# Hourglass attention and a gated MLP on one core: values by casting transfers, the k sums of batch 0 on TensorE, its norms in two parts

## The chip, the cores and the metric

The kernel runs on one core of a Trainium2 chip. Five engines work side by side from instruction lists of their own: TensorE (PE; its weight loads are listed apart as PEld), VectorE (DVE), ScalarE (ACT), GpSimd (POOL) and SyncE (SP). [...] Transfers run on 16 DMA engines, which all queues share. The metric is the time on the device in microseconds (us): the median of five runs of the kernel before is 329.76 us, with 327.95 as the lowest and 330.70 as the highest.

## The reference

```
q, k, v: 8 batches x 8 heads x 576 positions x 64, float32
q_d, k_d, v_d = means over 4 neighbouring positions (144 positions)
out_d   = softmax(q_d k_d^T / 8) v_d, each row repeated 4 times
out_loc = softmax over |i - j| < 4 of (q k^T / 8), times v
x       = out_d + out_loc, as 4608 tokens x 512
h       = x w_in            (512 -> 2048)
out     = (h * sigmoid(1.702 h)) w_out      (2048 -> 512)
```

So for every batch there are two attentions: one over all of a sequence shortened by four, and one over a band of seven positions. The MLP then takes all heads of a token together.

## The kernel before

The order of every engine is written out by hand: an instruction stands where its line is called, and nothing reorders it. The MLP is cut into nine groups of 512 tokens. A group is `mm1` (16 blocks of 128 hidden units, four matmuls of 128x512 each, L693) and then `mm2` (4 blocks of 128 tokens, 16 matmuls each, L749). While group g runs, the attention of batch g + 1 is put between its matmuls at numbered steps (`POS`, for group 0 `POS_0` and `VDP_0`). Steps from 16 on lie in `mm2`.

Before group 0 there is a lead-in: batch 0 must be loaded, attended and transposed before the first matmul of the MLP can start. It is written out at L787 to L890, and the change lies there and in the loads of batch 1.

- *Loads.* q and k come by DMAs of GpSimd's queue that cast float32 to bfloat16 (`load_1`, L202), 288 KB each as landed. The values of batch 0 come as float32 by ten DMAs of SyncE's queue (`load_v`, L222, two for each of five chunks) into the buffer `vf`, and VectorE casts each chunk into `vb` (`prep_v`, L319). A one-element copy on GpSimd (L812) reads chunk 2 of `vf`, and `w_in` (L255) is issued behind it, then q and k of batch 1, then the first half of `w_out` (L264). For batch 1, chunks 3 and 4 come by casting DMAs (`load_vb`, L233), and chunks 0 to 2 through `vf` with casts on GpSimd, with two more one-element copies as gates (L785, L907).
- *Transposes and sums of four.* VectorE transposes k and q (`prep_1`, L279) into `kT` and `qT`. GpSimd adds four neighbours in two steps (`pool_qk`, L304 and L313) into `kdT` and `qdT`; for the q of the second half of the heads VectorE does it in one reduction (`pool_q_reduce`, L293).
- *Scores.* `scores` (L384) are 80 small matmuls for the band of four heads, laid over a bar that `bar_others` (L365) writes. `scores_d` (L403) are 24 matmuls for the short attention, with `kdT` as the weights. ScalarE takes the exponentials (L414, L420, L832).
- *Averages.* `av_local0` (L523) and `av_down0` (L539) multiply by the values, for a pair of heads each; the values carry a column of ones, so the sums for the norm come along. The short values are sums of `vb` by TensorE (`prep_vd_pe`, L346), copied out by ScalarE (L355). `normalise0` (L552 to L557) is a reciprocal and two products on VectorE. `transp_sum` (L573, L584) transposes and adds the two attentions, and `copy_x` (L597 to L603) moves the result to `xT`.
- *Fillers.* `warm` (L649) are float32 matmuls whose result nobody reads. Each is carried out as two weight loads and two matmuls.
- *Start of the MLP.* `part` (L693) runs the matmuls of the first six hidden blocks as soon as each pair of heads is in `xT`.

PSUM holds three two-bank tiles (`PA[0]` to `PA[2]`) and two one-bank tiles (`PM`).

## Time and profile before

| What | Value |
|---|---|
| Median of 5 runs | 329.76 us |
| Profiled execution | 330.7 us, span 327.9 us |
| TensorE busy | 310.2 us (95%), 4962 weight loads |
| ScalarE, GpSimd, VectorE busy | 185.2, 138.0, 131.5 us |
| Granted TensorE clock | 1.000 of full speed |
| First matmul of hidden block 6 in group 0 (the lead-in is over) | 31.82 us |
| First long run of matmuls of group 1 | 66.16 us |

A busy TensorE is not TensorE at its peak, since the ends of its matmuls are modelled and fillers count as busy. Times in the text are counted from the start of the span. In the chain of waits each piece has a start, a length and what it was; "issue" is time in which an engine waited for nothing that the profile shows. In the list of instructions in order of time, a group has its start, its length, its line, what it wrote and read, and in brackets the idle time ahead of it.

### The profile page before, as it was taken

How to read it: one execution, taken by the hardware profiler on the slowest of the kernel's cores; microseconds unless marked ns; L12 is line 12 of the kernel's file. 1: busy time of each engine (PE TensorE's matmuls, PEld its weight loads, DVE VectorE, ACT ScalarE, POOL GpSimd, SP SyncE). 2: the span in 40 equal slices, each digit the busy share in tenths (PEclk: the TensorE clock that was granted, in tenths of full speed). 3: DMA queues.
4: the chain of work that ended last, by engine and by line, in shares of the span. 5: the costliest groups of instructions: out<-in, count | busy, mean ns of one | idle time of the engine just before them, and what ended most of it. 6: DMA issues, size and time to landing. Idle time of an engine off the chain costs nothing.

```text
span 327.9 us, 11050 instructions
## 1 busy us (share of the span) xinstructions
PE 310.2 (95%) x4908; PEld 159.0 (48%) x4962; DVE 131.5 (40%) x220; ACT 185.2 (56%) x322; POOL 138.0 (42%) x167
## 2 busy tenths in 40 slices
PE   8999979899999999999899999999999999999996
PEld 3564444445554554454544554445444544444444
DVE  6655332750676047703681267217730560000000
ACT  4645881566846582659267745775576646415611
POOL 7883851079306940496029901990098000000000
PEclk9999999999999999999999999999999999999999
DMA  7999999999917990699139942995190110011012
GB/s 125 182 191 209 189 128 196 187 193 252 173 68 153 203 161 36 151 205 185 46 108 184 175 116 72 185 207 125 55 155 3 65 39 32 0 66 64 0 54 75
DMA packets 63551, 41.08 MB, mean 125 GB/s; under 512 B 44048, under 2 KB 54416, under 8 KB 63504
## 3 DMA queue, kind: packets, MB, share of 16 engines
q1 hardware_dynamic: 52944, 26.42, 39.7%
q0 software_dynamic: 10416, 13.90, 25.0%
q8 instruction: 38, 0.62, 0.8%
q14 instruction: 9, 0.07, 0.1%
q10 hardware_dynamic: 144, 0.07, 0.1%
HBM read 44.83 MB, written 9.44 MB: 165 GB/s over the span
## 4 chain that ended last, share of the span: by engine, by line
PE 88%; DVE 5%; issue 4%; DMA 2%; ACT 1%; POOL 0%; ACTq 0%; DVEq 0%; POOLq 0%
PE pm L693 35%; PE pm L749 32%; PE pa L384 4%; PE pa L693 2%; PE pa L403 2%; PE pa L445 2%; PE pa L467 2%; DMA qb<-in_q_dram 2%; PE pa L749 2%; PE pa L498 2%; DVE xT L631 1%; PE pm L649 1%; PE pm L764 1%; DVE y L484 1%; DVE yl L557 1%
## 5 line engine op out<-in xcount | busy, mean ns | idle before, releaser
L693 PE MATMUL pm<-xT,w_in_bf 128*128 128x512 bf16 x528 | 120.3, 379 | 1.6 <-DVE xT L637 0.9
L749 PE MATMUL pm<-w_out_bf,gT 128*128 128x512 bf16 x493 | 114.1, 379 | 5.6 <-issue 5.5
L704 ACT ACTIVATE gT<-pm 128x512 bf16<-128x512 f32 x136 | 81.0, 598 | 46.1 <-PE pm L693 46.1
L693 PEld LDWEIGHTS <-w_in_bf 128*128 128x128 bf16 x576 | 55.6, 98 | 68.1 <-issue 1.9
L749 PEld LDWEIGHTS <-gT 128*128 128x128 bf16 x560 | 51.8, 98 | 59.6 <-issue 0.2
L304 POOL TENSOR_TENSOR pq<-kT 128x576 f32<-128x576 bf16 x16 | 18.5, 1158 | 98.0 <-DVE kT L279 97.9
L428 DVE TENSOR_TENSOR es<-es,mask 128x600 bf16<-128x600 bf16 x28 | 20.9, 762 | 90.3 <-ACT es L414 89.5
L734 ACT ACTIVATE osb<-pm 128x512 f32<-128x512 f32 (+2 forms) x35 | 20.8, 593 | 41.2 <-PE pm L749 37.3
L610 ACT COPY od<-pa 128x384 f32<-128x384 f32 (+1 forms) x56 | 18.4, 413 | 31.4 <-DVE y L484 18.7
L484 DVE TENSOR_TENSOR y<-pa,rc 128x896 bf16<-128x896 f32 x28 | 30.6, 1092 | 1.0
L631 DVE TENSOR_TENSOR xT<-pa,od 128x570 bf16<-128x570 f32 x28 | 21.1, 753 | 11.9 <-ACT od L610 11.5
L325 POOL TENSOR_TENSOR v<-v 112x512 f32<-112x512 f32 x18 | 22.8, 1265 | 0.0
L736 DVE TENSOR_SCALAR osb<-pm 128x128 f32<-128x128 f32 x1 | 0.3, 292 | 55.3 <-ACT osb L734 55.3
L414 ACT ACTIVATE es<-pa 128x600 bf16<-128x600 f32 x32 | 19.7, 668 | 2.5 <-PE pa L384 2.2
L279 DVE STREAM_TRANSPOSE kT<-kb 128x576 f32<-128x576 f32 x16 | 20.0, 1250 | 1.8 <-DMA kb<-in_k_dram 1.8
L279 DVE STREAM_TRANSPOSE qT<-qb 128x576 f32<-128x576 f32 x16 | 19.9, 1243 | 1.8 <-DMA qb<-in_q_dram 1.7
L304 POOL TENSOR_TENSOR pq<-qT 128x576 f32<-128x576 bf16 x15 | 17.2, 1146 | 0.0
L319 POOL CAST vb<-vf 128x2560 bf16<-128x2560 f32 (+1 forms) x9 | 16.1, 1810 | 0.0
L384 PEld LDWEIGHTS <-kT 32*64 32x64 bf16 x1280 | 12.1, 104 | 7.0 <-issue 5.6
L483 DVE RECIPROCAL rc<-pa 128x14 f32<-128x14 f32 x28 | 6.7, 241 | 21.3 <-PE pa L467 21.3
L420 ACT ACTIVATE ed<-pa 128x864 bf16<-128x864 f32 x15 | 13.5, 897 | 2.2 <-PE pa L403 2.2
L384 PE MATMUL pa<-qT,kT 32*64 32x60 bf16 x1280 | 14.1, 203 | 0.3 <-DVE qT L279 0.3
(104 smaller groups left out, 259.2 us busy)
## 6 DMA issues: line engine op xcount, KB each, us to landing
vf<-in_v_dram SPq DMA_DIRECT2D x76, 128.0 KB, 6.5
out_dram<-osb SPq DMA_DIRECT2D x35, 256.0 KB, 2.1
v<-in_v_dram SPq DMA_DIRECT2D x36, 192.0 KB, 5.4
kb<-in_k_dram POOLq DMA_DIRECT2D x16, 288.0 KB, 7.6
qb<-in_q_dram POOLq DMA_DIRECT2D x16, 288.0 KB, 8.8
w_out_bf<-in_moe_w_out_dram POOLq DMA_DIRECT2D x4, 512.0 KB, 13.4
w_in_bf<-in_moe_w_in_dram POOLq DMA_DIRECT2D x2, 512.0 KB, 7.5
w_in_bf<-in_moe_w_in_dram POOLq DMA_DIRECT2D x1, 1024.0 KB, 12.6
```

Of the source, the lines that this page charges most:

```text
L279: nc.vector.transpose(out=t32.rearrange("p (i c) -> p c i", c=18), in_=store[b, qd].bitcast(FP32).rearrange("p (c d) -> p c d", c=18),)
L304: nc.gpsimd.tensor_tensor(out=t1, in0=sv[:, :, 0:2, :], in1=sv[:, :, 2:4, :], op=ALU.add)
L325: eng.tensor_tensor(out=t1[0:112], in0=x[:, :, 0:2, :], in1=x[:, :, 2:4, :], op=ALU.add)
L384: nc.tensor.matmul(sp[r // 2][64 * par : 64 * par + 64, r % 2, 60 * i : 60 * i + 60], lhsT=kT[b, qd][rows, k0 : k0 + 64, a], rhs=qT[b, qd] ...
L414: nc.scalar.activation(out=es[2 * qd + u][:, :, 0:300], in_=sp[u][:, :, 0:300], func=AF.Exp, scale=inv_sqrt_d,)
L428: nc.vector.tensor_tensor(out=ev, in0=ev, in1=mask, op=ALU.mult)
L484: nc.vector.tensor_tensor(out=y[:, xs], in0=ov[:, :, :, 0:D], in1=rc[:, xs].to_broadcast([128, n, 7, D]), op=ALU.mult,)
L631: eng.tensor_tensor(out=sub(xT[hp], t0 + 3, (57, 2), (114, 5), (1, 57)), in0=sub(x, 3, (509, 2), (57, 5), (1, 57)), in1=sub(od, 3, (57, 2) ...
L693: nc.tensor.matmul(acc, lhsT=w_in_bf[:, dmc, ffc * 128 : (ffc + 1) * 128], rhs=xT[dmc][:, g * TG : g * TG + TG], start=(dmc == 0), stop=(d ...
L704: nc.scalar.activation(out=gT[:, ffc, :], in_=acc, func=AF.Silu, scale=GELU_SCALE)
L734: eng.activation(out=osb, in_=ap, func=AF.Copy, scale=1.0 / GELU_SCALE)
L749: nc.tensor.matmul(ops[t], lhsT=gT[:, ffc, t * 128 : (t + 1) * 128], rhs=w_out_bf[:, ffc, :], start=(ffc == 0), stop=(ffc == n_ffc - 1),)
```

## The change

The values of batches 0 and 1 all come by casting DMAs of GpSimd's queue straight into `vb`; `vf`, the casts and the gates of these two batches are gone. In batch 0 the sums of four over k are no longer formed: TensorE multiplies each of the four k rows by the summed q and adds the four products in PSUM (`scores_d0`, 96 matmuls in place of 24). The q sums of batch 0 are both reductions on VectorE. `normalise0` can run in two parts, "a" for the first four columns of results and "b" for the rest. Pairs 0, 1 and 2 are averaged side by side instead of 0 and 1 first, most fillers are taken out, and two steps of group 0 stand earlier.

```diff
+    def scores_d0(qd, sd):
+        bank = banks(sd)
+        for kc in range(3):
+            for a in range(2):
+                for f in range(4):
+                    for r in range(4):
+                        rows = slice(32 * r, 32 * r + 32)
+                        j = r % 2
+                        k0 = 192 * kc + f
+                        nc.tensor.matmul(
+                            bank[r // 2][64 * j : 64 * j + 64, SD * kc : SD * kc + SD],
+                            lhsT=kT[0, qd][rows, k0 : k0 + 253 : 4, a],
+                            rhs=qdT[0, qd][rows, :, a],
+                            start=(a == 0 and f == 0), stop=(a == 1 and f == 3),
+                            tile_position=(32 * r, 64 * j),
+                        )
+        return sd
...
-    POS_0 = [16, 18, 27, 54, 68, 60, 76]
-    VDP_0 = 52
+    POS_0 = [16, 18, 27, 50, 68, 60, 76]
+    VDP_0 = 46
...
-    load_v(0, gate=after(kdT[1][0:1, SD, 0:1], nc.vector))
+    for i in range(5):
+        load_vb(0, i)
+    load_w_in(0, 512)
+    load_w_in(512, 512)
+    load_w_in(1024, 1024)
+    for qd in range(NQ):
+        load_qk(1, qd)
+    load_w_out(0)
+    load_w_out(1)
...
-    pool_qk(0, 0)
-    sp = scores(0, 0, barred=True)
+    sp = scores(0, 0, barred=True, sp=PA[0:2])
     exp_local(0, sp)
     prep_1("k", 0, 1)
+    pool_q_reduce(0, 0)
     prep_1("q", 0, 1)
     pool_q_reduce(0, 1)
-    pool_qk(0, 1, "k")
...
-    for i in range(5):
-        prep_v(0, nc.vector, i=slice(i, i + 1))
     warm(2)
-    sd = scores_d(0, 0)
-    exp_down(0, sd)
-    sp = scores(0, 1, barred=True)
+    exp_down(0, scores_d0(0, PA[2]))
+    sp = scores(0, 1, barred=True, sp=PA[0:2])
     exp_local(1, sp)
-    for hp in range(2):
-        o[hp] = PA[hp]
-    warm(1)
-    scores_d(0, 1, PM)
+    scores_d0(1, PM)
...
+    for i in (range(3), range(3, 4)):
+        for hp in range(3):
+            av_local0(hp, o[hp], i)
+    for hp in range(3):
+        normalise0(o[hp], y[hp], "a")
+    prep_vd_pe(0, PM[0], range(0, 2))
+    prep_vd_pe(0, PM[1], range(2, 3))
     nc.scalar.preload_act_table_set("silu_and_others")
-    warm(1, t=PA[2][:, 0, :])
...
+    for hp in range(3):
         av_local0(hp, o[hp], range(4, 5))
-    prep_vd_pe(0, pm_tile(), range(2, 3))
-    warm(1, 256)
-    for hp in range(2):
+        if hp == 0:
+            warm(1, 256, PM[0])
         av_down0(hp, o[hp])
-        y[hp] = normalise0(o[hp])
...
-    warm(1)
-    warm(1, 256)
+        normalise0(o[hp], y[hp], "b")
+    warm(1, t=PM[0])
...
         if g == 0:
             nc.gpsimd.memset(v4[32:64], 0.0)
+            load_vb(1, 0)
+            load_vb(1, 1)
+            prep_qk(1, 0)
+            pool_qk(1, 0)
+            load_vb(1, 2)
+            prep_qk(1, 1)
+            pool_qk(1, 1)
             load_vb(1, 3)
             load_vb(1, 4)
-            load_v(1, gate=after(qf[1, 1][0:1, 0:1], nc.vector), chunks=range(3))
...
             load_w_out(2)
             load_w_out(3)
-            for i in range(3):
-                prep_v(1, nc.gpsimd, i=slice(i, i + 1))
             for qd in range(NQ):
                 load_qk(2, qd)
-            loads_2()
+            load_v(2, gate=after(w_out_bf[0:1, 12, 0:1], nc.gpsimd))
+            load_v4(2)
```

The k tiles of batch 0 are made 64 positions longer, and VectorE clears the tail, so that the strided weights of `scores_d0` stay inside the tile.

## The prediction

> **What bounds the kernel now.** I began with the page's first part, then the chain of waits in order of time, then TensorE's weight loads and VectorE's list, and last the DMA view in short windows.

> ```profile
> PE 310.2 (95%) x4908; PEld 159.0 (48%) x4962; DVE 131.5 (40%) x220; ACT 185.2 (56%) x322; POOL 138.0 (42%) x167
> ...
> q8 instruction: 38, 0.62, 0.8%
> ```

> TensorE is the bound: from 66.16 us, where group 1 gets going, the chain runs from matmul to matmul. The change leaves that stretch alone. So it can move the end only by moving the lead-in (to 31.82) and group 0 (to 66.16). The lead-in in the chain, with start, length and work:

> ```profile
> 9.57 1.91 PE pm L649 x4
> 11.48 0.51 PE pa L403 x24
> 11.99 0.62 PE pa L365 x4
> 12.61 0.84 PE pa L384 x79
> 13.46 1.05 PE pm L649 x2
> 14.51 0.44 PE pm L403 x17
> 14.95 0.21 issue
> 15.16 0.32 PE pm L403 x7
> ...
> 31.82 0.21 PE pm L693
> ```

> VectorE's norms of the first pairs of heads stand in the list by time:

> ```profile
> 20.98 0.25 DVE L552 RECIPROCAL rc<-pa 128x14 f32<-128x14 f32 x1 [2.83 <-PE pa L539]
> 21.26 0.42 DVE L553 TENSOR_TENSOR yd<-pa,rc 128x256 bf16<-128x256 f32 x1
> 21.60 0.95 DVE L557 TENSOR_TENSOR yl<-pa,rc 128x768 bf16<-128x768 f32 x1
> ```

> Now the pause at 14.95: 0.21 us in the middle of 24 equal matmuls, for nothing. A far longer one lies in group 0:

> ```profile
> 46.49 0.43 PEld L403 LDWEIGHTS <-kdT 32*64 32x64 bf16 x24 [1.74 <-issue]
> ```

> What this line waits for in the code (`kdT`, `qdT`, the exponential that frees PSUM) was done by 44.42. I counted TensorE's weight loads up to each unexplained pause. The pauses at 14.95, 44.66, 60.14, 121.38 and 156.31 (0.21 to 1.8 us) come after 224, 735, 991, 2014 and 2654 loads. From the first they are 511, 767, 1790 and 2430 on: multiples of 128, two off at most. Each load has one matmul, so it is every 256 instructions, and 2 x 4962 instructions over the 38 packets of the instruction queue is 261 per packet. TensorE waits there for its own instruction list.

> In quarter-microsecond windows those packets start at 12.25, 17.5, 24.25, 30.5, 43.25, 51.0, 58.25 and 62.25; TensorE passes block borders (256 instructions) at 11.4, 15.16, 21.0, 27.6, 40.9, 46.49, 54.7 and 60.8. One packet per border, fetched one block ahead. Border to packet takes 2.4, 3.4 and 3.05 us at 15 to 30 us, while weights stream in; packet to release 2.4 to 3.2 us. Where the next border had to wait, border to release was 4.1 (122.07), 4.7 (157.40), 5.6 (46.49) and 6.0 us (60.77).

> [...] the new weights of L403's successor step by 4 positions of 4 bytes, `kdT` by 4 bytes. [...]

> **The change part by part, for the lead-in.**

> *Values.* Ten casting DMAs follow the iotas on GpSimd at 6.33; one issue takes 0.68 (24.86, L233), so the last is out at 13.1. Landed by what? In 38.5 to 39.0 the engines moved 513 such packets, a whole DMA of 512 in 0.48 us, so ten need 4.8 behind q and k (about 8.9): the data is in by about 15, the last landed near 16. TensorE needs chunk 4 after 18. The five casts (0.43 each) leave VectorE. Cost on the path: nothing, 2 us of cover. `w_in` is issued at 13.1 instead of 14.58; batch 1's loads follow about 3 us earlier, also covered: TensorE waited for none of them before. With six values DMAs more, GpSimd still issues the second half of `w_out` by 42.5 (44.6 before).

> *k sums.* Six GpSimd operations go (three of 1.15 + 0.67). VectorE gets a reduction of 1.35 and two small clears: transpose of kT1 to about 10.0, reduction to 11.35. The filler ends at 11.48, so no wait. `scores_d0` is 96 matmuls for 24. Such a piece took 0.51 for 24 and 0.39 for 23 later: 17 to 21 ns each, so 1.6 to 2.0 us, 3.3 if the 16-byte step doubles it; I take 1.8. Twice 1.8 for 0.51 and 0.76 is +2.3.

> *Fillers.* From 13.46 on 1.05, 1.06, 0.84, 0.63, 0.63 and 1.5 go; 0.63 and 1.05 stay: -4.0.

> *Norms.* VectorE's products cost 1.03 ns an element ((0.95 - 0.42)/512). Part "a" is 0.28 + 0.61, "b" 0.27 + 0.34 + 0.34 by starts: 5.5 us for three pairs, 4.4 before, but "a" starts 3.5 us sooner.

> *Without the instruction list* the sum runs: scores_d0 11.5 to 13.3; bar and scores (0.62, 0.84) to 14.8; scores_d0 to 16.6; averages (48 x 16 ns) to 17.4; short values (0.69 + 0.28) to 18.4; VectorE's "a" 17.4 to 20.1, "b" to 23.0; last filler to 21.65; transposes (0.73 each), pair 3 (0.66) and 24 matmuls of 0.216 end at 30.4. That is 1.4 before 31.82. The two earlier steps in group 0 I cost at nothing: the same matmuls, their values in by 43; if late, TensorE would pause by that delay.

> *With it.* The new matmuls are 144 pairs, and five fillers fewer take out 20 instructions: +268 instructions in the lead-in, and where 9.6 us passed between the borders at 11.4 and 21.0, the code now wants 5.6. Border at load 224 is reached at 14.15 (28 pairs into the second scores), released as before at about 15.15: 1.0 lost. The next border lies 76 matmuls into the second scores_d0, reached at 17.1; released 15.15 + 2.4 + 2.4 = 19.95: 2.85 lost. Rest, exponentials, averages and "a" follow; the third lies in the short averages of pair 1, reached at 23.7, released 19.95 + 3.4 + 2.4 = 25.75: 2.05 lost. The fourth lies in pair 3's transposes, reached at 31.8, released at 25.75 + 5.4 = 31.15. From 25.75: rest of pairs 1 and 2 0.5, filler 1.05, transposes, pair 3 and first matmuls 5.0 to 32.2, the last 18 matmuls 3.9: 36.1. That is 4.3 later than 31.82. (The three losses make 5.9; VectorE's waits hide 0.2 of it.) Bounds: 4.1 us per block gives +1.1; 6.3 gives +6.5.

> *After it.* Group 0 meets its borders again inside both scores of batch 1, 256 instructions in about 3.8 us, as before (1.8 lost both times). Later borders move 11 instructions along the code: with the 4 us per block that fits the pauses seen there, +0.3 at most. I put 0.

> **The rivals.** (1) The blocks come faster than 5 us: GpSimd's small value packets, then w_in, are other traffic than before. At 4.1 us, +1.1: 330.9. For it: 4.1 and 4.7 measured later; against: 2.4 and 3.4 from border to packet in this very traffic. (2) The list never holds TensorE up, and the kernel gains 1.4: 328.4. It decides at the 2.9 us that TensorE takes from load 224 to load 352: below that nothing waits. Against: nothing under 4.1 was seen where a border waited; for: 256 instructions passed in 3.4 to 3.6 at 221 to 228 us without a pause over 0.25. (3) All as forecast, and a pause of about 3 us drops TensorE's clock[...], or weights at the 16-byte step are slow: +2.5 more, 336.6. Against: [...]slow weights hide behind the fetch.

> **How the numbers follow.** The profiled execution took 330.7 with a span of 327.9; 2.8 lie around the span. Its 330.7 stands 0.9 over the median. A shift carries to both, so I add 4.3 to the median: 334.1. Chances: forecast 0.62, (1) 0.22, (2) 0.08, (3) 0.08. One per cent is 3.3 us, about what a measurement tells from no change. Of the forecast's spread (+2.5 to +6.5) some 0.07 lies under 3.3. So slower 0.63, same 0.35, faster 0.02, since even (2) stays within 1%. Range: from (1)'s lower end to (3)'s middle, 330.2 to 337.0; 2 is left out with half of (3).

> **What would show it.** Pauses in TensorE with "issue" as the reason after about 224, 352 and 480 weight loads, the middle one 2 to 4 us inside the second scores_d0; instruction packets at about 17.5 and 23; first matmul of block 6 near 36; group 1 near 70.5; no wait for values or weights. It is wrong if the pauses are under 1 us, or if VectorE or a value DMA ends the waits there.

## The result, and the profile after

The changed kernel takes 331.77 us (median of 28 runs, 329.44 to 332.85); the kernel before, run beside it, 328.64. The ratio is 1.008, with a 95% interval of 1.0063 to 1.0096: slower by 2.6 us (3.1 between the medians), where 4.3 were forecast. The median lies in the forecast range of 330.2 to 337.0; the loss of over one per cent, which was given the best chance, did not come. One profiled execution of each kernel is thin for so small a difference, so each was profiled a second time later on (`e13_before2`, `e14_after2` below). By stages, from the chains of waits:

| us | before | before, 2nd | after | after, 2nd |
|---|---|---|---|---|
| lead-in, to the first matmul of hidden block 6 | 31.82 | 31.32 | 37.20 | 38.92 |
| group 0, from there to group 1 | 34.34 | 33.97 | 31.72 | 32.27 |
| from group 1 to the end of the span | 261.7 | 260.1 | 260.0 | 260.0 |
| profiled execution | 330.7 | 327.2 | 330.7 | 333.0 |

Mean against mean: the lead-in is 6.5 us longer, group 0 is 2.2 shorter, the rest 0.9 shorter; the profiled executions differ by 2.9. So a larger loss than forecast stands against a gain that was not forecast at all. In the list by time the first matmul of block 6 stands 0.16 us earlier than in the chain; times below that come from the list are marked so.

The page of the changed kernel, busy time and the instruction queue:

```profile
PE 310.6 (94%) x5042; PEld 162.3 (49%) x5096; DVE 129.3 (39%) x222; ACT 185.0 (56%) x322; POOL 141.0 (43%) x173
...
q8 instruction: 40, 0.66, 0.8%
```

134 weight loads more, and two packets of instructions more. Its chain of waits (start, length, work):

```profile
11.06 3.04 PE pa L425 x95
...
15.48 2.30 PE pm L425 x74
17.79 3.01 issue
20.80 0.82 PE pm L425 x20
...
25.93 0.79 issue
...
32.52 0.40 issue
...
37.20 1.73 PE pm L722 x8
...
50.19 0.42 issue
```

`scores_d0` (L425) takes 3.04 us for 95 matmuls, 32 ns each, where 17 to 21 had been taken. In the middle of the second one TensorE stops for 3.01 us for nothing that the profile shows, after 352 weight loads, and again after 480 and 608: each 128 weight loads with their matmuls, or 256 instructions, from the last. (The page's 5042 matmuls and 5096 loads over 40 packets of the instruction queue are 253 per packet.) In the second execution the pauses stand at the same first two places (3.07 and 1.57 us). The pause in the scores of batch 1 at 50.19 is what is left of the 1.74 us of before.

VectorE's norms, in the list by time, now begin with part "a":

```profile
22.29 0.21 DVE L580 RECIPROCAL rc<-pa 128x8 f32<-128x8 f32 x1 [8.84 <-PE pa L545]
22.53 0.69 DVE L587 TENSOR_TENSOR yl<-pa,rc 128x512 bf16<-128x512 f32 x1
...
25.82 0.20 DVE L580 RECIPROCAL rc<-pa 128x6 f32<-128x6 f32 x1 [0.91 <-PE pa L561]
```

They start later than before's 20.98, since they wait for averages (L545) behind the long pause. TensorE itself waits for no transfer of values or weights. One-microsecond windows of the changed kernel show what goes on during the pause and after it (after the busy times of the five engines the last three columns are the granted clock, the DMA share and GB/s):

```profile
17.00:18.00 1.00, 0.79 (x27) 0.65 (x24) 0.00 (x0) 0.00 (x0) 1.00 (x3) 1.00 1.20 197
18.00:19.00 1.00, 0.00 (x0) 0.00 (x0) 0.00 (x0) 0.00 (x0) 0.53 (x1) 1.00 1.22 207
...
22.00:23.00 1.00, 1.00 (x30) 0.84 (x20) 0.67 (x2) 0.61 (x2) 1.00 (x1) 0.50 1.16 219
```

Some 200 GB/s of weights stream throughout, and 1.2 us after the end of the pause the granted clock drops to 0.50 for 3.4 us, to 25.4.

### The profile page after: what moved, and what is told of

It is laid out like the page before. It is cut to its first block, busy times and chain, and to the rows that moved or that the text cites. A ratio compares the mean times of both kernels' runs of the same rounds, so it can differ in the third digit from the quotient of the medians.

```text
span 328.9 us, 11290 instructions
## 1 busy us (share of the span) xinstructions
PE 310.6 (94%) x5042; PEld 162.3 (49%) x5096; DVE 129.3 (39%) x222; ACT 185.0 (56%) x322; POOL 141.0 (43%) x173
## 3 DMA queue, kind: packets, MB, share of 16 engines
q0 software_dynamic: 18864, 14.95, 32.3%
## 4 chain that ended last, share of the span: by engine, by line
PE 91%; issue 4%; DVE 3%; POOL 1%; ACT 0%; POOLq 0%; ACTq 0%
PE pm L722 35%; PE pm L778 34%; PE pa L388 4%; PE pa L722 2%; PE pa L467 2%; PE pa L407 2%; PE pa L520 2%; PE pa L778 2%; PE pa L489 1%; PE pm L678 1%; PE pm L793 1%; PE pm L425 1%; DVE xT L660 1%; PE pa L425 1%; PE pm L350 0%
## 5 line engine op out<-in xcount | busy, mean ns | idle before, releaser
L308 POOL TENSOR_TENSOR pq<-kT 128x576 f32<-128x576 bf16 x14 | 16.2, 1157 | 94.5 <-DVE kT L283 94.5
L450 DVE TENSOR_TENSOR es<-es,mask 128x600 bf16<-128x600 bf16 x28 | 19.5, 709 | 93.9 <-ACT es L436 93.0
L639 ACT COPY od<-pa 128x384 f32<-128x384 f32 (+1 forms) x56 | 18.3, 414 | 31.4 <-DVE y L506 22.4
L660 DVE TENSOR_TENSOR xT<-pa,od 128x570 bf16<-128x570 f32 x28 | 21.1, 753 | 11.4 <-ACT od L639 11.4
L436 ACT ACTIVATE es<-pa 128x600 bf16<-128x600 f32 x32 | 19.7, 668 | 2.7 <-PE pa L388 2.5
L308 POOL TENSOR_TENSOR pq<-qT 128x576 f32<-128x576 bf16 x14 | 16.0, 1146 | 0.0
L234 POOL DMA_DIRECT2D vb<-in_v_dram x20 | 13.7, 704 | 5.3 <-DMA w_in_bf<-in_moe_w_in_dram 3.8
L332 POOL TENSOR_TENSOR vd<-v 112x256 bf16<-112x256 f32 x18 | 13.7, 759 | 1.4
```

The lines of the kernel that those rows point to most:

```text
L308: nc.gpsimd.tensor_tensor(out=t1, in0=sv[:, :, 0:2, :], in1=sv[:, :, 2:4, :], op=ALU.add)
L436: nc.scalar.activation(out=es[2 * qd + u][:, :, 0:300], in_=sp[u][:, :, 0:300], func=AF.Exp, scale=inv_sqrt_d,)
L450: nc.vector.tensor_tensor(out=ev, in0=ev, in1=mask, op=ALU.mult)
L660: eng.tensor_tensor(out=sub(xT[hp], t0 + 3, (57, 2), (114, 5), (1, 57)), in0=sub(x, 3, (509, 2), (57, 5), (1, 57)), in1=sub(od, 3, (57, 2) ...
```

## Experiments

Ratios are to the kernel before, run beside each; the changed kernel stands at 1.008. "Border" is the place in TensorE's list where a block of 256 instructions ends, as the pauses after 352, 480 and 608 loads mark it; "lag" is the time from passing a border to the instruction queue's next packet in the trace. The pause and idle times are those of the matmuls.

### Is it the instruction list?

**Shift the borders.** 128 instructions more ahead of everything:

```diff
-    warm(4)
+    warm(2)
+    for _ in range(68):
+        nc.tensor.matmul(
+            PM[0][0:4, 0:4], lhsT=es[0][:, 0, 300:304], rhs=es[0][:, 0, 300:304],
+            start=True, stop=True,
+        )
```

> The changed kernel with 128 more instructions on TensorE ahead of all its other work: two of the four first fillers (each 512 columns) give way to 68 tiny matmuls (128 x 4 by 128 x 4) with their weight loads; nothing else is changed. Every border of 256 instructions then lies 64 weight loads earlier in the code. Theory A (TensorE waits for its own instruction list): the 3.4 us pause leaves the 76th matmul of the second scores_d0; pauses now stand at about the 12th matmul of that piece, then at or just before psel, in the averages between, and about 10 row-column pairs into the scores of batch 1, each 256 instructions after the last, 4 to 6.5 us from border to release. Total within 2 us of the changed kernel. Rival B (the pause belongs to that matmul: a PSUM bank, the exponential before it, the k or q data): the pause stays at the 76th matmul of the second scores_d0, 3 us long, whatever the instruction count.

Measured, in TensorE's list by time:

```profile
16.80 0.59 PE L425 MATMUL pm<-qdT,kT 32*64 32x144 bf16 x11
17.58 2.75 PE L425 MATMUL pm<-qdT,kT 32*64 32x144 bf16 x85 [0.19 <-issue]
20.25 0.60 PE L545 MATMUL pa<-vb,es 64*64 64x65 bf16 x43
23.77 0.32 PE L545 MATMUL pa<-vb,es 64*64 64x65 bf16 x5 [2.92 <-issue]
```

The pause has left the 76th matmul of the second `scores_d0`. A short one stands ahead of the 12th, the long one in the averages just ahead of psel (the name in the traces for the matmuls of the short values, `prep_vd_pe`), where the next border now is: theory A in the place, and rival B is out, for that matmul, its PSUM bank and its data are what they were. From border to release the first took 3.2 us, its packet coming 0.88 us after the border, ahead of the weights; the second took 6.2. The size was missed. The ratio is 1.0209 (1.0138 to 1.0279), 4.2 us over the changed kernel and not within 2, and the profile shows the clock at 0.50 twice, from 8.7 to 12.1 us, when the tiny matmuls had just run, and for 10 us from 22.4; no pause came in the scores of batch 1.

**The step of the weights.**

```diff
-                            lhsT=kT[0, qd][rows, k0 : k0 + 253 : 4, a],
+                            lhsT=kT[0, qd][rows, k0 : k0 + 64, a],
```

> The changed kernel, but scores_d0 reads its 64 weight columns side by side (step 4 bytes) in place of every fourth position (step 16 bytes). This sums the wrong k rows and leaves the k sums out; the count of instructions, their shapes and their order are the same. Both theories: a matmul of scores_d0 goes from 32 ns to 17 to 21 ns, so the first piece (96) from 3.1 to about 1.8 us, the second from about 3 us of work to 1.8. Theory A (instruction list is the limit): the time that the piece gives back is lost at the borders; a pause of 0.5 to 1.3 us comes up after 224 weight loads, the release of the block that begins in the second scores_d0 comes at 19.5 to 21 us as before, and the kernel's time falls by at most 0.5 us. Rival C (the slow weights are what made the lead-in longer): the lead-in ends 2 to 3 us earlier and the kernel's time falls by 2 to 3 us.

The instructions of L425 in the changed kernel (name, count, and ns as least, median and most):

```profile
L425 PEld LDWEIGHTS <-kT x192: 188/211/212, 11.0 to 21.3; 32*64 32x64 bf16 x192
```

and with the weights side by side:

```profile
L425 PEld LDWEIGHTS <-kT x192: 102/103/172, 11.0 to 19.3; 32*64 32x64 bf16 x192
```

So the step of 16 bytes doubles a weight load (211 ns against 103), and the first piece goes from 3.11 to 1.74 us. The doubling is the bound of 3.3 us that the prediction set beside its 1.8. The ratio falls to 1.0028 (1.0007 to 1.0049), 1.7 us less than the changed kernel: more than theory A's 0.5 and less than rival C's 2. The expected pause after load 224 was only 0.15 us; at load 352 the pause grew to 3.55, and the block was released at 18.90 instead of 20.80, 5.4 us after its border where 19.5 to 21 had been expected. The release is tied to when the border is passed, and that came 1.2 us sooner. Of those 1.9 us the lead-in kept 0.8 (36.37), and the clock stood at 0.50 from 18.3 to 28.6.

**k sums back on VectorE.** A new `k_reduce` writes `kdT` by a reduction in the form of `pool_q_reduce`; behind each half's q sum (the first half's q sum moves ahead of the second half's transposes):

```diff
+    k_reduce(0, 0)
...
+    k_reduce(0, 1)
...
-    exp_down(0, scores_d0(0, PA[2]))
+    exp_down(0, scores_d(0, 0, PA[2]))
...
-    scores_d0(1, PM)
+    scores_d(0, 1, PM)
```

> The changed kernel with one part of the change taken back: batch 0's k sums of four come from one VectorE reduction per half (the same form as the q sums), and the scores against them are the 24 matmuls of scores_d, not the 96 of scores_d0. That is 288 TensorE instructions fewer; values, norms in two parts, order of group 0 stay as changed. Theory A (instruction list): the lead-in's pauses shrink to under 1 us each, the first matmul of block 6 comes at 30 to 32.5 us (37.2 in the changed kernel), and the kernel is 3 to 6 us faster than the changed one, so 0.5 to 3 us faster than the kernel before. Rival D (the lead-in got longer through VectorE's norms in two parts or the values' arrival, not through the new matmuls): the lead-in ends at 35 us or later and the time stays within 1.5 us of the changed kernel's.

Its chain of waits (lines stand 8 further down than in the changed kernel):

```profile
20.97 1.39 issue
22.36 0.35 PE pa L569 x13
```

One pause of 1.39 us is left (under 1 was expected), the first matmul of block 6 comes at 32.15, group 0 takes 31.66, and the ratio is 0.9959 (0.9935 to 0.9983): 4.0 us faster than the changed kernel and faster than the one before. Rival D is out: with this one part taken back the loss is gone. The edit takes out the slow weights and the instructions at once, so it doesn't tell what each of them cost; the step of the weights above bears on the first, the tiny matmuls below on the second.

**That part alone, in the kernel before.** `scores_d0` with its zeroed tail put into the kernel before, GpSimd's k sums of batch 0 taken out:

```diff
-    pool_qk(0, 0)
+    pool_qk(0, 0, "q")
...
-    pool_qk(0, 1, "k")
...
-    sd = scores_d(0, 0)
+    sd = scores_d0(0, ps_tile())
...
-    scores_d(0, 1, PM)
+    scores_d0(1, PM)
```

> The kernel before with one part of the change alone: batch 0's k sums of four by TensorE (scores_d0 with its zeroed tail, 288 instructions more), GpSimd's six k additions gone; values, norms, fillers and order as before. Theory A: the lead-in ends 4 to 6 us later than before's 31.82 us, with pauses of issue after loads 224, 352 and 480, the middle one the longest, and the kernel is 4 to 6 us slower than before: ratio 1.012 to 1.018. If the other parts of the change cost a part of the loss themselves, it is less than 3 us, ratio under 1.009.

The ratio is 1.0178 (1.0121 to 1.0234) and the lead-in ends at 36.83: the size as expected, the reason not. TensorE's list by time:

```profile
16.47 3.10 PE L425 MATMUL pm<-qdT,kT 32*64 32x144 bf16 x96
19.50 1.12 PE L671 MATMUL pa<-wz 128*128 128x512 f32 x2
```

There is no pause in the second `scores_d0`. Two such pieces of 3.10 us for 0.51 and 0.76 are +4.9 us, and that is nearly all of the lead-in's 5.0. With the old fillers in between, the next border is reached only at 18.63 us, 2.6 us after its block's packet. In the changed kernel the fillers are gone, TensorE gets there earlier, and the list holds it up instead. That the two limits cost about the same here is read from one profile of each.

### What makes a block late?

**No weights while it is fetched.** `w_in` and all loads behind it in the queue wait for the exponential of the second `scores_d0`; the block of calls moves to behind this line:

```diff
+    nc.gpsimd.tensor_copy(out=w_in_bf[0:1, 0, 0:1], in_=eds[1][0:1, 0, 0:1])
```

> The changed kernel with w_in, batch 1's q and k and the first half of w_out held back on GpSimd until the exponential of the second scores_d0 is done (about 20 us), in place of being issued from 13.1 us on. Between 16 and 20 us the core then moves next to nothing but instructions. Theory G (the block fetch takes 6 us from border to release because its packet stands in line behind weight traffic): from the border at load 224 to the release inside the second scores_d0 3.0 to 4.5 us (6.05 in the changed kernel), pause there at most 1.5 us (3.0). Rival H (the fetch takes its time whatever else moves): 5.3 to 6.5 us and a pause of 2.5 to 3.5. Both: w_in then arrives too late, TensorE waits for it in the first blocks, and the kernel's time says nothing on the question.

One-microsecond windows while the block is fetched:

```profile
16.00:17.00 1.00, 1.00 (x40) 1.00 (x40) 0.00 (x0) 0.77 (x2) 0.00 (x0) 1.00 0.00 0
17.00:18.00 1.00, 0.79 (x27) 0.65 (x24) 0.00 (x0) 0.00 (x0) 0.00 (x0) 1.00 0.00 0
```

Nothing moves. The packet itself, in the DMA view, first from 18.25 to 18.75 us in the changed kernel and then from 15.5 to 16 us here (queue, packets, MB, share of 16 engines; q0 is GpSimd's queue):

```profile
q0 software_dynamic: 100, 0.10, 121.2%
q8 instruction: 1, 0.02, 12.2%
...
q8 instruction: 1, 0.02, 16.1%
```

TensorE's list behind the border, which is passed at 14.75 us as in the changed kernel:

```profile
18.33 0.82 PE L425 MATMUL pm<-qdT,kT 32*64 32x144 bf16 x21 [0.54 <-issue]
```

The packet comes 0.95 us after the border (3.77 in the changed kernel), the release 2.6 us after the packet (2.3): border to release 3.6 instead of 6.05, pause 0.54 instead of 3.01, the clock at 1.00 throughout. Theory G: the weights delay the block's packet. Block 6 starts at 32.68 (in the list; 37.03 there in the changed kernel). What was saved is lost in group 0, where TensorE waits for `w_out` (0.92 and 1.66 us) and pauses at two borders (1.25 and 1.17); one run took 330.85.

**The same gate, short.** The loads wait for the first `scores_d0`'s exponential instead:

```diff
+    nc.gpsimd.tensor_copy(out=w_in_bf[0:1, 0, 0:1], in_=eds[0][0:1, 0, 0:1])
```

> The changed kernel with w_in and the loads behind it held on GpSimd only until the exponential of the first scores_d0 is done (about 15.0 us, in place of issue from 13.1), so that the instruction block asked for at the border of 14.75 us gets its packet before the weights start to stream (lag 0.95 us as in e5_gate, 3.8 in the changed kernel). Theory G (weight traffic ahead of the block's packet makes the pause): border to release at load 352 3.3 to 4.3 us (6.05 in the changed kernel), pause under 1.3 us, TensorE's clock stays at 1.00, first matmul of block 6 at 33 to 35.5 us (37.20), and the kernel is 1.5 to 4 us faster than the changed one: ratio to before 0.996 to 1.004. Rival M (the traffic only shifts the loss to the next border): first matmul of block 6 at 36 or later, ratio 1.006 to 1.010.

```profile
18.62 0.83 PE L425 MATMUL pm<-qdT,kT 32*64 32x144 bf16 x21 [0.64 <-issue]
...
24.54 0.22 PE L561 MATMUL pa<-vd,ed 48*64 48x65 bf16 x2 [1.85 <-issue]
```

That is TensorE's list by time: the first pause is 0.64 (border to release 3.7), but the next block, fetched among the weights (lag 3.64), comes 5.9 us after its border. Block 6 starts at 35.78, a little past the 35.5 expected; the ratio is 1.0012 (0.9992 to 1.0032), 2.2 us faster than the changed kernel. Both are partly right: the traffic makes the pause, and some of what is saved is lost at the next border. That the clock would stay at 1.00 was wrong: it fell to 0.50 from 25.9 to 29.3, after a pause of 1.85 us.

### The norms, the clock, and a faster version

**Norms in one part again**, on the kernel with k sums on VectorE:

```diff
-    for hp in range(3):
-        normalise0(o[hp], y[hp], "a")
...
-        normalise0(o[hp], y[hp], "b")
+        normalise0(o[hp], y[hp])
```

> The kernel with the k sums taken back to VectorE (e3_ksum), with one more part of the change taken back: the norms of the first three pairs run in one part each, after their last average, as before the change. Theory K (norms in two parts shorten the lead-in, as forecast by their earlier start): VectorE begins them 3 us later, the first matmul of block 6 comes 1 to 2.5 us later than 32.15 us, and the kernel is 1 to 2.5 us slower than with the k sums alone taken back. Rival L (the split is hidden: fewer and longer products are as good): within 0.5 us.

The ratio is 0.9974 (0.9952 to 0.9997), against 0.9959 with two parts; block 6 starts at 32.19 against 32.15. VectorE begins the norms at 20.72 instead of 17.10. Rival L: the split is worth nothing that can be told there. TensorE pauses 1.5 us at the border behind these averages in any case (1.4 with two parts).

**24 tiny matmuls more**, in a wait for VectorE of the same kernel:

```diff
+    for _ in range(24):
+        nc.tensor.matmul(
+            PM[0][0:4, 0:4], lhsT=es[1][:, 0, 300:304], rhs=es[1][:, 0, 300:304],
+            start=True, stop=True,
+        )
     sp = scores(0, 1, barred=True, sp=PA[0:2])
```

> The kernel with the k sums taken back to VectorE (e3_ksum), plus 24 tiny matmuls (128 x 4 by 128 x 4, PM[0][0:4, 0:4]) with their loads where TensorE waits 1.0 us for VectorE, just ahead of the second scores. It adds work and takes none away. Theory A (instruction list): the border that lay 20 pairs into the second scores_d (passed at 16.1 us, after VectorE's wait) now lies near the end of the second scores (passed at about 14.0); the next block is released about 2 us earlier, at 20 to 20.5 in place of 22.36, the pause of 1.4 us there shrinks below 0.5 or goes, the later borders come within 16 instructions of where they lie in the changed kernel, and the kernel is 1.0 to 3.0 us faster than with the k sums alone taken back: ratio to before 0.987 to 0.993. Rival I (the list is not the limit there; the pause follows VectorE's values or the clock): no gain, ratio 0.995 to 0.998.

The ratio is 0.9884 (0.9849 to 0.9919), 2.1 us below the version without them by the medians (325.34 and 327.44). The kernel got faster by work that nobody needs: the border is passed at 13.9 instead of 16.1, ahead of VectorE's wait, and the fetch runs during that wait. TensorE's list shows the wait, and the pause that is left further on:

```profile
15.98 0.86 PE L415 MATMUL pm<-qdT,kdT 32*64 32x144 bf16 x24 [1.82 <-DVE kdT L304]
...
26.43 0.59 PE L730 MATMUL pa<-xT,w_in_bf 128*128 128x512 bf16 x2 [0.83 <-issue]
```

The pause of 1.39 at load 352 is gone. This is the clearest evidence for theory A, since all else that was changed is more work.

**Fillers against the clock drop.** 20 tiny ones, and:

```diff
+    warm(1, 256, PM[0])
     sp = scores(0, 1, barred=True, sp=PA[0:2])
     exp_local(1, sp)
+    warm(1, 512, PM[1])
     scores_d(0, 1, PM)
```

> As e6_tiny, but 20 tiny matmuls, a filler of 256 columns beside them and one of 512 columns in the next wait for VectorE (1.8 us), so that TensorE does not stand idle between 12.2 and 15.9 us. Instruction borders lie where e6_tiny has them, give or take 4. Theory J (the granted clock fell to 0.50 from 17 to 20.7 us with the k sums taken back, because TensorE had been idle, and that costs the psel matmuls 0.8 and the filler 0.6 us): clock 1.00 throughout the lead-in, psel's 14 matmuls 0.9 in place of 1.7 us, and 0.5 to 1.4 us faster than e6_tiny. Theory A alone (the next block's release binds there): the time won is lost in the pause at the next border, and the kernel is within 0.4 us of e6_tiny.

The same microsecond of the kernel with k sums on VectorE:

```profile
18.00:19.00 1.00, 1.00 (x12) 0.50 (x8) 0.96 (x4) 0.61 (x2) 0.33 (x1) 0.50 1.22 201
```

and with the fillers:

```profile
18.00:19.00 1.00, 0.80 (x10) 0.54 (x6) 0.97 (x4) 0.98 (x3) 0.29 (x1) 1.00 1.15 181
```

The clock stays at 1.00 and psel takes 0.99 us instead of 1.71, yet the ratio is 0.9898 (0.9856 to 0.994), no better than 0.9884. The time won comes back as a pause of 0.55 us at load 352 and 0.91 at load 480 (none and 0.83 with the tiny matmuls only), and the lead-in ends just 0.25 us earlier than with those. Theory A, for the lead-in. In group 0 this profile also has a wait of 0.93 us for `w_out`, so the time of the whole kernel alone would not have told.

**With the gate at about 15.5 us** (behind `exp_local(1, sp)`, reading `es[1]`):

```diff
+    nc.gpsimd.tensor_copy(out=w_in_bf[0:1, 0, 0:1], in_=es[1][0:1, 0, 0:1])
```

> e7_warm (k sums back on VectorE, 20 tiny matmuls and two fillers in the waits) with w_in and the loads behind it held until the exponential of the second scores is done (about 15.5 us in place of 13.1). Theory G: the pause of 0.55 us at 19.7 goes, since its block's packet no longer waits behind weights; the lead-in ends 0.4 to 0.9 us earlier; ratio to before 0.984 to 0.990. Rival N (w_in, batch 1's keys or w_out then come too late and TensorE waits for them in group 0, as it did by up to 1.7 us in e5_gate): 0.3 us or more slower than e7_warm, ratio 0.991 to 0.996.

The ratio is 0.9864 (0.9831 to 0.9897), 324.52 us: the fastest of all, 4.5 us under the kernel before. The pause at load 352 is gone and block 6 starts at 30.29, 0.9 before that of the version without the gate (31.18; both in the list). The gain over that version is inside the intervals.

### Why did group 0 get shorter?

**The two steps back**, in the changed kernel:

```diff
-    POS_0 = [16, 18, 27, 50, 68, 60, 76]
-    VDP_0 = 46
+    POS_0 = [16, 18, 27, 54, 68, 60, 76]
+    VDP_0 = 52
```

> The changed kernel with the two steps of group 0 put back to their old places (POS_0's fourth entry 54 in place of 50, VDP_0 52 in place of 46). Theory E (the 2.6 us that group 0 got shorter come from these two steps, through a wait on y and the average behind it that went away): group 0 is 0.7 to 1.5 us longer, and the kernel 0.7 to 1.5 us slower than the changed one. Rival F (group 0 got shorter because the instruction list had more time to run ahead in the long lead-in, so that its first two pauses shrank from 1.8 and 1.3 us to 0.6 and 0): group 0 is within 0.4 us of the changed kernel's.

Group 0 takes 32.68 instead of 31.72, +0.96 (+0.41 against the second look at the changed kernel); the ratio is 1.0122 (1.0088 to 1.0157). TensorE's list has a line again that the kernel before has too (first line: before, second look; second line: this run):

```profile
56.75 0.35 PE L498 MATMUL pa<-id,y 60*64 60x60 bf16 x20 [0.73 <-DVE y L484]
...
63.08 0.35 PE L520 MATMUL pa<-id,y 60*64 60x60 bf16 x20 [0.72 <-DVE y L506]
```

Theory E: with the old places the transposes wait 0.72 us for VectorE's `y`; in the two looks at the changed kernel they wait for nothing and for 0.23 us.

**The two steps alone**, in the kernel before (the same two lines, the other way round):

> The kernel before with one part of the change alone: the two steps of group 0 moved earlier (POS_0's fourth entry 50 for 54, VDP_0 46 for 52). With the changed kernel's loads this was worth 0.96 us of group 0. If it is worth the same by itself: group 0 0.6 to 1.2 us shorter than the kernel before's in e13_before2, ratio 0.996 to 0.999. If batch 1's values come too late for the earlier steps with the old order of loads, TensorE waits for them and the gain is gone: ratio 0.999 to 1.004.

The wait on `y` (0.73 us in `e13_before2`) is gone, group 0 takes 32.41 against 34.14 (both from the list), the ratio is 0.9986 (0.9963 to 1.0009). Of the 1.7 us in the profile, 0.9 is less pause at two borders (0.55 and 0.29 against 1.32 and 0.43), which moves from execution to execution. The values of batch 1 were in time. In the time itself the gain is 0.5 us and not told from nothing.

**The traffic at the border.** The block that starts in the scores of batch 1 is asked for one border earlier: its packet starts at 43.34 us in the kernel before and at 47.44 in the changed one, and it is released at 46.49 and 50.61. When the kernel before passes that border, at 40.92 us, the values of batch 1 stream as float32 in SyncE's queue (q1), as its DMA view from 42 to 43 us shows; in the changed kernel, which passes it at 46.25, hardly anything moves just ahead of it (second line: the last columns are clock, DMA share and GB/s):

```profile
q1 hardware_dynamic: 741, 0.18, 134.0%
...
45.00:46.00 1.00, 1.00 (x36) 0.43 (x35) 0.00 (x0) 0.73 (x2) 1.00 (x3) 1.00 0.10 7
```

The packet comes 2.42 and 1.20 us after the border. To try it with other traffic, in the changed kernel, `w_out`'s second half ahead of the last values:

```diff
+            load_w_out(2)
+            load_w_out(3)
             load_vb(1, 3)
             load_vb(1, 4)
-            load_w_out(2)
-            load_w_out(3)
```

> The changed kernel with the second half of w_out issued ahead of the last four value transfers of batch 1 in group 0, at about 44.4 us in place of 47.1, so that weights stream when TensorE passes the border at about 46.2 us; the four value transfers follow at 46. Theory G (group 0 got shorter because the loads around this border moved: in the changed kernel 0 to 7 GB/s flow up to 46 us and the packet comes 1.2 us after the border, in the kernel before 183 GB/s and 2.4 us): the packet comes 2 to 4 us after the border, the pause inside the scores of batch 1 grows from 0.42 to 1.2 to 2.5 us, group 0 takes 32.5 to 34 us from its first matmul of block 6 to group 1 (31.72 in the changed kernel), and the kernel is 0.5 to 2 us slower than the changed one: ratio to before 1.009 to 1.014. Rival F (the pause shrank for another reason, say that the border lies elsewhere in the code): pause within 0.3 us of 0.42, ratio 1.006 to 1.010.

```profile
56.28 0.23 PE L388 MATMUL pa<-qT,kT 32*64 32x60 bf16 x6 [2.59 <-issue]
```

In TensorE's list the pause of 0.42 is now 2.59 us: the border is passed at 49.74, the packet comes 4.14 us later (1.20 in the changed kernel), with 98 to 193 GB/s from 50 us on. Group 0 takes 33.89, 2.2 longer than in the first look and 1.6 longer than in the second. Theory G: traffic at this border makes the pause. The ratio, 1.0199 (1.0169 to 1.0229), is more than was expected: the lead-in, which the edit doesn't reach, ended at 40.70 in this profile, after a pause of 3.97 us and 13.7 us at half clock. Why it fared worse there was not settled.

**Second looks at both kernels.**

> The kernel before once more, for a second profiled execution. Its first one took 330.7 us against a median of 328.6. If group 0's 34.34 us (pauses of 1.66 and 0.44 us at two borders) belong to the kernel, group 0 takes 34.0 to 34.6 us again and the first matmul of block 6 comes at 31.5 to 32.3; if they were the chance of that execution, group 0 takes 32.3 to 33.6 us, with a first pause under 1.3 us and a second under 0.2, and the span is 325 to 326.5 us.

> The changed kernel once more, for a second profiled execution. If its lead-in's 37.20 us and group 0's 31.72 belong to the kernel: 36.7 to 38 and 31.5 to 32.0, half clock for 3 us or more after the pause at load 352, and the pauses at the same instructions. If they were chance, the lead-in ends under 36 or over 38.5.

Group 0 of the kernel before takes 33.97, at the lower edge of the first range, with a pause of 1.32 us, so most of its length belongs to the kernel; block 6 comes at 31.32, a little ahead of the range, and the span of 325.4 us fits the second; what was chance was 1.6 us from group 1 on (border pauses of 0.47, 0.19, 0.87 and 0.37 us in the first execution, one of 0.22 in the second). The changed kernel keeps its pauses (3.07 and 1.57), halves its clock twice for 3.4 us, and ends the lead-in at 38.92, above the first range; group 0, 32.27, lies above it too. The places of the pauses belong to the kernel, their sizes vary.

## Why the prediction was right or wrong, point by point

- *Direction and mechanism of the lead-in: right.* TensorE is held up by its own list at places 256 instructions apart, after the 352nd, 480th and 608th load (3.01, 0.79 and 0.40 us). Shifting the borders, thinning the list, adding tiny matmuls and moving the weights out of the way each moved the pauses as this says.
- *Values: right.* No wait for them in either look. *Weights "also covered": wrong.* Nobody waited for them, but they delayed the blocks: behind the border at load 224 the packet came after 3.77 us, not 2.4, and a kernel that holds them back for 2 us is 2.2 us faster (`e9_short`).
- *`scores_d0` at 1.8 us: wrong in size.* 3.04, near the bound of 3.3. Border at load 224 was therefore passed at 14.75, and the 1.0 us expected there fell away. The sum without a list, with the measured price, is 30.4 + 2 x (3.04 - 1.8) = 32.9; with the weights out of the way 32.68 was measured (in the list), and a pause of 0.54 us is in that.
- *Load 352, 2.85 us: 3.01, in part by luck.* The block came 0.85 us later than forecast, by the late packet, and TensorE got there 0.7 later, by the slow weights. Load 480, 2.05: 0.79 and 1.57, as TensorE got there later. Its release came 5.9 and 6.5 us after the border (5.8 expected). Load 608: 0.40 in the first look where none was expected.
- *The lead-in, +4.3: 5.4, and 7.6 in the second look.* Too low by the slow weights and the late packets; in the second look a second stretch at half clock lies in it (a filler of 512 columns took 2.07 us there, 1.12 in the first). How much of the rest is the clock's was not separated.
- *Norms in two parts, and a start 3.5 us sooner: wrong.* They started later; where they could start sooner, the split gave nothing.
- *Group 0, "The two earlier steps in group 0 I cost at nothing" and "(1.8 lost both times)": this is the step that failed.* Group 0 is 2.2 us shorter in the mean of both looks, where nothing was put. The steps end a wait on `y` of 0.73 us. The pause in the scores of batch 1 is 0.42 and 0.52 us instead of 1.66 and 1.32: the float32 values that streamed at its border are gone by the change itself. The prediction had listed the lags under traffic, and had then not asked what streams at this border after the change. Its place for the second half of `w_out`, 42.5, was wrong as well: it was issued at 47.12, since GpSimd waited 4.51 us for VectorE's transpose of batch 1's k; weights at this border would have brought the pause back, as `e12c_wout` shows. Not all of the pause's change can be put down to the loads: in `e15_steps`, with the old loads, it was 0.55 us. In the measured terms the sum is +6.5 - 2.2 - 0.9 = +3.4 in the span, +2.9 in the profiled executions, +2.6 in the ratio: without the gain in group 0 the loss would have been above the forecast, not below.
- *Later borders, 0:* -0.9 in the mean, nearly all of it from border pauses in one execution of the kernel before.
- *The rivals.* (1), 4.1 us per block, is near what a block took with the weights held back (3.6 and 3.7), not in this kernel. (2), no hold-up, is out. (3) came true in part: slow weights were not hidden behind the fetch (1.7 us came back without them), and the clock did halve. Half clock followed pauses of 3.01 us (changed kernel), 1.85 (`e9_short`) and 1.57 (`e14_after2`). But none followed the 2.59 us of `e12c_wout` or the 1.66 of the kernel before, so the length of a pause alone doesn't decide. In the changed kernel the halving took psel from 0.99 (with the clock at 1.00) to 1.71 us and a filler from 0.70 to 1.22; `e7_warm` suggests that this lay largely in the shadow of the next block.

## What to carry to other kernels

Many small matmuls cost their instructions too: where code passes 256 of TensorE's instructions in less time than a block takes to arrive (here 3.2 to 3.7 us from border to release with the weights out of the way, in `e1_shift`, `e5_gate` and `e9_short`, and 5.4 to 6.5 among them), count the borders and price what the DMA engines carry at each of them. A border can be moved into a wait that is there anyway, by a few tiny matmuls (24 in `e6_tiny`, for 2.1 us). And when transfers are reordered, look again at every border, not only at who reads the data.
